# Reworking the head of a fused state-space and dense kernel: another load queue, a square root with a reciprocal, transposed tiles copied by two engines

## The chip, the cores and the metric

One core of one Trainium2 chip. Times are device microseconds of one execution. Every execution quoted here was undisturbed ("fast"). A kernel was timed in 4 to 6 executions, with 6 to 11 executions of the kernel before beside it. Ratios are the mean time of one kernel's fast runs over that of the kernel before in the same rounds, so they are not quite the ratio of the medians that stand beside them.

The device time is longer than the span of the trace (first to last instruction). The part outside the span hardly varies within a kernel: about 2.0 us for the kernel before.

## The reference, cut to what matters

```python
xn = layernorm(x)                                   # x: 1 x 2048 x 1024
# A: a diagonal state-space layer on xn; the recurrence over 2048 steps is complex
Bu = einsum("bld,pd->blp", xn, B_bar);  h_t = Lam_bar * h_(t-1) + Bu_t
A  = 2 * einsum("blp,dp->bld", h, C).real + xn * Dskip
# B: a dense layer with mish: 1024 -> 3584 -> 1024
Bo = mish(xn @ w1 + b1) @ w2
out = x + A + Bo
```

The output is bf16. The layernorm feeds both halves, so no useful matmul can start before the first rows are normalized and transposed.

## The kernel before

The program keeps one list of instructions for each engine, in program order, and derives semaphores from recorded reads and writes. The 2048 rows are done in four blocks of 512 rows. In each block PE does w1 (28 tiles `f`, 8 matmuls each), then the projection into the state (8 tiles `j`, 16 matmuls each), then w2 and the projection out. The first block also has to make what later blocks reuse: sine and cosine tables, transposed B and C, coefficients.

The head (rows `q` = 0 and 1 are the ones that the first half-width matmuls wait for):

```python
for q in range(NQ):
    load_x(SP, 0, q)                       # 4 tiles of 128 rows, all on SyncE's queue
# ... 4 small parameter rows on ScalarE's queue, then 7 weight tiles (512 KB each) on SyncE's ...
def first_rsqrt(q):                        # ScalarE: 1/sqrt estimate
    aop(lambda e: e.activation(rc(q, 1), mv[:, q, 1:2], AF.Abs_reciprocal_sqrt, ...))
def first_apply(q):                        # VectorE: one Newton step (3 small ops), then xn
    ...
keep_busy(34)                              # filler matmuls (0.107 us each, 0.056 us from 6.5 us on)
PE.op(... transpose of the parameter rows ...)
keep_busy(16)
# ... statistics of tile 0 on VectorE, of tile 1 on ScalarE ...
first_apply(0); first_transpose(0); keep_busy(6)
first_apply(1); first_transpose(1); keep_busy(8)
first_copy(0, VE); first_copy(1, VE)       # PSUM -> xnT, both on VectorE
```

GpSimd makes the phases of the sine tables, 24 instructions in a row, and in their middle issues the x tiles of the second block:

```python
for j in range(NJ):
    phases(j)        # px = iot*thp; py = round(px); xs = px - py: 128x512 fp32 each
    if j == 3:
        for q in range(NQ):
            load_x(PO, 1, q)               # block 1, GpSimd's queue
```

Of the kernel before, what the change touches and what calls it, by code (L numbers as in the profile page):

```python
# [5 lines left out]
ALU = mybir.AluOpType  # L6
AF = mybir.ActivationFunctionType
DT = mybir.dt

P = 128  # L10
# [146 lines left out]
def build_kernel(nc, A_x, A_Lambda_re, A_Lambda_im, A_B_re, A_B_im, A_C_re, A_C_im,  # L157
                 A_log_dt, A_Dskip, B_w1, B_b1, B_w2, out):
    bf16, f32, i32 = DT.bfloat16, DT.float32, DT.int32
    S, D = A_x.shape[1], A_x.shape[2]  # L160
# [4 lines left out]
    NQ = TB // P  # L165
    NK = D // P
    NJ = NP // P
    NF = F // P
# [4 lines left out]
    EPS = 1e-5  # L173

    PE = Queue(nc, "pe")
    VE = Queue(nc, "ve")
    AC = Queue(nc, "ac")
    PO = Queue(nc, "po")
    SP = Queue(nc, "sp")

    def sb(name, shape, dtype):
        return nc.alloc_sbuf_tensor(name, shape, dtype)
# [18 lines left out]
    hT = sb("hT", [P, 2, NJ, TB], bf16)  # L201
    b_hT = [[Buf("hT%d_%d" % (ci, j)) for j in range(NJ)] for ci in range(2)]
    xnT = sb("xnT", [P, NK, TB], bf16)
    b_xnT = [Buf("xnT%d" % q) for q in range(NQ)]
    s_xnT = [DmaSem(nc, "d_xnT%d" % q) for q in range(NQ)]
    tab = sb("tab", [P, 2, NJ, TB], bf16)
    b_tab = [Buf("tab%d" % j) for j in range(NJ)]
# [4 lines left out]
    xn = sb("xn", [P, NQ, D], bf16)  # L212
    b_xn = [Buf("xn%d" % q) for q in range(NQ)]
# [4 lines left out]
    NST = 3 * NJ + NF  # L218
    st = sb("st", [NST, P], bf16)
    b_st = Buf("st")  # L220
    ident = sb("ident", [P, P], bf16)
    b_ident = Buf("ident")
    par = sb("par", [P, NST], f32)
    b_par = Buf("par")
    stats = sb("stats", [P, 2, 2, 6], f32)
    b_stats = [Buf("stats%d" % i) for i in range(2)]
    mv = sb("mv", [P, NQ, 2], f32)
    b_mv = [Buf("mv%d" % i) for i in range(NQ)]
    rs = sb("rs", [P, NQ, 4], f32)
    b_rs, b_rs1, b_rs2 = ([Buf("rs%s%d" % (n, i)) for i in range(NQ)] for n in "abc")  # L230
    kon = sb("kon", [P, 3], f32)
    b_kon = Buf("kon")
    CN = ["dt", "a", "th", "thp", "r", "xs", "ys", "xc", "yc", "s1", "c1", "lr", "li", "nr",
# [15 lines left out]
    b_ps = [Buf("ps%d" % i) for i in range(8)]  # L249

    def ps16(i):
        return ps[:, i, :].bitcast(bf16)
# [23 lines left out]
    vop, aop, pop = VE.op, AC.op, PO.op  # L276


    s_st = DmaSem(nc, "d_st", nper=4)
# [4 lines left out]
    def load_x(queue, blk, q):  # L284
        r0 = blk * TB + q * P
        i = blk % 2
        queue.dma(lambda e: e.dma_start(xx[:, i, q, :], A_x[0, r0:r0 + P, :]),  # L287
                  s_xx[i][q] if blk else s_x0[q], writes=[b_xx[i][q]])

    for q in range(NQ):  # L290
        load_x(SP, 0, q)
    for src, r0, n in ((A_log_dt, 2 * NJ, NJ), (A_Lambda_im, NJ, NJ), (A_Lambda_re, 0, NJ),
                       (B_b1, 3 * NJ, NF)):
        AC.dma(lambda e, src=src, r0=r0, n=n: e.dma_start(
            st[r0:r0 + n, :], src.rearrange("(j p) -> j p", p=P)), s_st, writes=[b_st])


    items = []
# [27 lines left out]
                                  compare_op=ALU.is_equal, fill=0.0), reads=[b_ident], writes=[b_ident])  # L326
    for n, v in enumerate((HALF_PI, 0.0, EPS)):
        pop(lambda e, n=n, v=v: e.memset(kon[:, n:n + 1], v), reads=[b_kon], writes=[b_kon])
    pop(lambda e: e.iota(iot_i[:], pattern=[[1, TB]], base=0, channel_multiplier=0), writes=[b_iot_i])
    pop(lambda e: e.tensor_copy(iot[:], iot_i[:]), reads=[b_iot_i], writes=[b_iot])  # L330

# [4 lines left out]
    def rc(q, n):  # L336
        return rs[:, q, n:n + 1]

    def first_sums_v(q, h):
        s = q // 2  # L340
        vop(lambda e: e.bn_stats(stats[:, s, h, :], xx[:, 0, q, h * 512:(h + 1) * 512]),  # L341
            reads=[b_xx[0][q]], writes=[b_stats[s]])

    def first_var_v(q):
        s = q // 2
        vop(lambda e: e.bn_aggr(mv[:, q, :], stats[:, s, :, :]), reads=[b_stats[s]], writes=[b_mv[q]])
        vop(lambda e: e.tensor_scalar(rc(q, 0), mv[:, q, 1:2], EPS, None, op0=ALU.add),
            reads=[b_mv[q]], writes=[b_rs[q]])

    def first_mean_a(q):  # L350
        aop(lambda e: e.activation(sq[:], xx[:, 0, q, :], AF.Identity, bias=kon[:, 1:2], accum_out=rc(q, 3)),
            reads=[b_xx[0][q], b_kon], writes=[b_sq, b_rs[q]])
        aop(lambda e: e.activation(mv[:, q, 0:1], rc(q, 3), AF.Copy, scale=-1.0 / D),
            reads=[b_rs[q]], writes=[b_mv[q]])

    def first_var_a(q):
        aop(lambda e: e.activation(sq[:], xx[:, 0, q, :], AF.Square, bias=mv[:, q, 0:1], accum_out=mv[:, q, 1:2]),
            reads=[b_xx[0][q], b_mv[q]], writes=[b_sq, b_mv[q]])

    def first_rsqrt(q):  # L360
        scale = 1.0 if q % 2 == 0 else 1.0 / D
        aop(lambda e: e.activation(rc(q, 1), mv[:, q, 1:2], AF.Abs_reciprocal_sqrt, scale=scale, bias=kon[:, 2:3]),
            reads=[b_mv[q], b_kon], writes=[b_rs1[q]])

    def first_apply(q):

        v, y, t = (rc(q, n) for n in range(3))
        if q % 2:
            vop(lambda e: e.tensor_scalar(v, mv[:, q, 1:2], 1.0 / D, EPS, op0=ALU.mult, op1=ALU.add),
                reads=[b_mv[q]], writes=[b_rs[q]])  # L370
        vop(lambda e: e.scalar_tensor_tensor(out=t, in0=y, scalar=y, in1=v, op0=ALU.mult, op1=ALU.mult),  # L371
            reads=[b_rs[q], b_rs1[q]], writes=[b_rs2[q]])
        vop(lambda e: e.tensor_scalar(t, t, -0.5, 1.5, op0=ALU.mult, op1=ALU.add),
            reads=[b_rs2[q]], writes=[b_rs2[q]])
        vop(lambda e: e.tensor_tensor(y, y, t, op=ALU.mult), reads=[b_rs1[q], b_rs2[q]], writes=[b_rs1[q]])
        vop(lambda e: e.tensor_scalar(xn[:, q, :], xx[:, 0, q, :], mv[:, q, 0:1], y,  # L376
                                      op0=ALU.subtract if q % 2 == 0 else ALU.add, op1=ALU.mult),
            reads=[b_xx[0][q], b_mv[q], b_rs1[q]], writes=[b_xn[q]])

    def first_transpose(q):  # L380
        bank = 6 + q % 2
        for k in range(NK):
            PE.mm(lambda e, k=k: e.transpose(ps16(bank)[:, k * P:(k + 1) * P], xn[:, q, k * P:(k + 1) * P], ident[:]),  # L383
                  reads=[b_xn[q], b_ident], writes=[b_ps[bank]], first=k == 0, last=k == NK - 1)

    def first_copy(q, queue):
        dst = xnT[:, :, q * P:(q + 1) * P]
        srcp = ps16(6 + q % 2).rearrange("p (k t) -> p k t", k=NK)
        if queue is AC:
            aop(lambda e: e.copy(dst, srcp), reads=[b_ps[6 + q % 2]], writes=[b_xnT[q]])  # L390
        else:
            vop(lambda e: e.tensor_copy(dst, srcp), reads=[b_ps[6 + q % 2]], writes=[b_xnT[q]])  # L392


    rv = [sb("rv%d" % i, [P, NQ], f32 if i < 3 else i32) for i in range(4)]
# [60 lines left out]
    def keep_busy(n):  # L456
        for i in range(n):
            PE.mm(lambda e: e.matmul(ps[:, 4, 0:P], lhsT=ident[:], rhs=ident[:], start=True, stop=True),
                  reads=[b_ident], writes=[b_ps[4]], first=i == 0, last=i == n - 1)

    keep_busy(34)
    PE.op(lambda e: e.transpose(ps16(5)[:, 0:NST], st[:, :], ident[0:NST, 0:NST]),
          reads=[b_st, b_ident], writes=[b_ps[5]])
    keep_busy(16)
    aop(lambda e: e.activation(rs[:, :, 3], kon[:, 2:3].to_broadcast([P, NQ]), AF.Abs_reciprocal_sqrt, bias=kon[:, 2:3]),
        reads=[b_kon], writes=b_rs)
    for h in range(2):
        first_sums_v(0, h)
    first_var_v(0)
    first_sums_v(2, 0)  # L470
    first_mean_a(1)
    first_rsqrt(0)
    first_var_a(1)
    first_rsqrt(1)
    first_apply(0)
    first_transpose(0)
    keep_busy(6)
    first_apply(1)
    first_transpose(1)
    keep_busy(8)  # L480
    first_copy(0, VE)
    first_copy(1, VE)
    first_mean_a(3)
    first_var_a(3)
    first_rsqrt(3)
    first_sums_v(2, 1)
    first_var_v(2)
    first_rsqrt(2)
    first_apply(2)
    first_apply(3)  # L490
    vop(lambda e: e.tensor_copy(par[:, :], ps16(5)[:, 0:NST]), reads=[b_ps[5]], writes=[b_par])
    NSPLIT = 6

    def first_half(f, half):
        s, fi = f // 2, f % 2
        wt = ring[:, s, :].rearrange("p (k f) -> p k f", k=NK)
        ts = slice(half * 256, half * 256 + 256)
        for k in range(NK):
            PE.mm(lambda e, k=k: e.matmul(ps[:, f, ts], lhsT=wt[:, k, fi * P:(fi + 1) * P], rhs=xnT[:, k, ts],  # L499
                                          start=k == 0, stop=k == NK - 1),  # L500
                  reads=[b_ring[s]] + b_xnT[2 * half:2 * half + 2], writes=[b_ps[f]],
                  first=half == 0 and k == 0, last=half == 1 and k == NK - 1)

    for f in range(NSPLIT):
        first_half(f, 0)
        if f in (2, 3):
            q = f
            first_transpose(q)
            first_copy(q, AC if q == 2 else VE)

    aop(lambda e: e.activation(c("dt"), ldt, AF.Exp), reads=[b_par], writes=[b_cs["dt"]])
    small("a", "dt", lre, ALU.mult)
# [358 lines left out]
```

## Time and profile before

| what | before |
|---|---|
| median of the first 3 executions | 626.24 us (625.97 to 626.64) |
| span of the profiled one | 623.9 us |
| first useful matmul | 10.27 us |
| PE's only longer wait after it | 1.5 us, at 94.55 us |

From the page of the kernel before: the span, the busy time of the engines, the chain of work that ended last, and PE's group of w2 matmuls. In a group the columns are busy us and mean ns of one, then the idle time ahead of them and what ended it.

```profile
span 623.9 us, 7415 instructions
...
PE 616.7 (99%) x2961; PEld 287.4 (46%) x2961; DVE 466.0 (75%) x695; ACT 247.1 (40%) x162; POOL 50.0 (8%) x47
...
PE 95%; DVE 3%; DMA 1%; issue 0%; SPq 0%; DVEq 0%
...
L715 PE MATMUL ps<-ring,act 128*128 128x512 bf16 x896 | 194.2, 379 | 1.5 <-DVE mt L666 1.5
```

The last one: once, PE waits 1.5 us for VectorE.

The timeline of the head before (start, duration, engine, line, operation, output and inputs, idle time before it):

```profile
0.79 1.84 SPq L287 DMA_DIRECT2D xx<-in_A_x_dram  x4
...
1.41 3.81 PE L458 MATMUL ps<-ident 128*128 128x128 bf16 x34 [1.41 <-POOL kon L328]
...
6.81 0.55 DVE L376 TENSOR_SCALAR xn<-xx,mv,rs 128x1024 bf16<-128x1024 bf16 x1
...
7.41 0.62 PE L383 MATMUL ps<-ident,xn 128*128 128x128 bf16 x8 [0.50 <-DVE rs L369]
...
8.17 0.55 DVE L376 TENSOR_SCALAR xn<-xx,mv,rs 128x1024 bf16<-128x1024 bf16 x1
...
8.63 1.49 DVE L392 COPY xnT<-ps 128x1024 bf16<-128x1024 bf16 x2
...
8.77 0.62 PE L383 MATMUL ps<-ident,xn 128*128 128x128 bf16 x8 [0.40 <-DVE xn L376]
...
10.27 2.78 PE L499 MATMUL ps<-xnT,ring 128*128 128x256 bf16 x24 [0.43 <-DVE xnT L392]
```

Fillers, then xn0, its transposes, xn1, its transposes, two copies of 0.7 us, and the first useful matmul at 10.27 us.

### The profile page before, as it was taken

To read this page: it belongs to the slowest core of one execution; us is meant where nothing else is said; L and a number is where in the kernel's file an instruction comes from. 1 tells how busy PE (TensorE), PEld (TensorE's weight loads), DVE (VectorE), ACT (ScalarE), POOL (GpSimd) and SP (SyncE) were. 2 spreads that over 40 slices of the span, in tenths; PEclk is the share of its full clock that TensorE was granted. 3 is DMA by queue.
4 is the path that set the end of the run, shared out by engine and by line. 5 is a ranking of instruction groups with operands and counts; after the bars stand their busy time and mean duration, and the time that the engine had idled before them with its cause. 6 is when DMAs were issued, how large, how long until landed. Compare 5 with 4: busy or idle time off the path is not lost.

```text
span 623.9 us, 7415 instructions
## 1 busy us (share of the span) xinstructions
PE 616.7 (99%) x2961; PEld 287.4 (46%) x2961; DVE 466.0 (75%) x695; ACT 247.1 (40%) x162; POOL 50.0 (8%) x47
## 2 busy tenths in 40 slices
PE   8999999999999999999999999999999999999998
PEld 7644444444444444444444444444444444444443
DVE  6799999999457599999047759999624856999603
ACT  6679995441059950000008992000001999000000
POOL 1899000000100000000010000000000000000000
PEclk9999999999999999999999999999999999999999
DMA  9999976750365400764065520285204532033001
GB/s 268 215 259 249 258 152 172 200 166 3 106 198 169 134 2 7 232 171 132 13 190 144 159 101 1 77 227 153 85 35 134 167 137 68 1 131 106 1 0 68
DMA packets 124188, 79.41 MB, mean 127 GB/s; under 512 B 48890, under 2 KB 106490, under 8 KB 124154
## 3 DMA queue, kind: packets, MB, share of 16 engines
q1 hardware_dynamic: 120656, 71.58, 42.9%
q10 hardware_dynamic: 2538, 4.21, 1.8%
q0 software_dynamic: 960, 3.15, 1.8%
q8 instruction: 24, 0.39, 0.3%
q14 instruction: 10, 0.08, 0.0%
HBM read 63.19 MB, written 4.19 MB: 108 GB/s over the span
## 4 chain that ended last, share of the span: by engine, by line
PE 95%; DVE 3%; DMA 1%; issue 0%; SPq 0%; DVEq 0%
PE ps L715 48%; PE ps L641 29%; PE ps L661 16%; DVE mt L666 2%; PE ps L499 2%; DMA xx<-in_A_x_dram 1%; DVE hT L669 0%; PE ps L383 0%; DVE hT L671 0%; DVE xn L376 0%; SPq L287 0%; DVE xnT L392 0%; DVE xx L752 0%; DVE rs L371 0%; DVE stats L341 0%
## 5 line engine op out<-in xcount | busy, mean ns | idle before, releaser
L715 PE MATMUL ps<-ring,act 128*128 128x512 bf16 x896 | 194.2, 379 | 1.5 <-DVE mt L666 1.5
L641 PE MATMUL ps<-xnT,ring 128*128 128x512 bf16 x848 | 183.7, 379 | 0.0
L619 ACT ACTIVATE act<-hb 128x3584 bf16<-128x3584 bf16 x16 | 50.9, 3183 | 246.2 <-DVE hb L648 245.9
L715 PEld LDWEIGHTS ps<-ring,act 128*128 128x128 bf16 x896 | 87.5, 98 | 107.6 <-DVE mt L666 2.0
L641 PEld LDWEIGHTS ps<-xnT,ring 128*128 128x128 bf16 x848 | 82.9, 98 | 99.9
L648 DVE TENSOR_SCALAR hb<-ps,par 128x512 bf16<-128x512 f32 x112 | 82.8, 747 | 55.3 <-PE ps L641 54.0
L661 PE MATMUL ps<-xnT,BT 128*128 128x512 bf16 x512 | 111.2, 379 | 0.0
L715 PE MATMUL ps<-CT,hT 128*128 128x512 bf16 x512 | 111.2, 379 | 0.0
L666 DVE TENSOR_TENSOR mt<-ps,tab 128x1024 bf16<-128x1024 f32 x64 | 75.4, 1219 | 13.2 <-PE ps L661 11.7
L661 PEld LDWEIGHTS ps<-xnT,BT 128*128 128x128 bf16 x512 | 50.0, 98 | 60.5
L715 PEld LDWEIGHTS ps<-CT,hT 128*128 128x128 bf16 x512 | 50.0, 98 | 60.5
L752 DVE TENSOR_TENSOR xx<-ps,xx 128x1024 bf16<-128x1024 f32 (+1 forms) x17 | 19.5, 1161 | 72.0 <-PE ps L715 72.0
L681 DVE TENSOR_TENSOR_SCAN hT<-cs,qi,hT 128x512 bf16<-128x512 f32 x48 | 58.9, 1269 | 0.0
L621 ACT ACTIVATE act<-act 128x3584 bf16<-128x3584 bf16 x16 | 51.0, 3190 | 0.2
L620 ACT ACTIVATE act<-act 128x3584 bf16<-128x3584 bf16 x16 | 51.0, 3190 | 0.2
L686 DVE TENSOR_TENSOR mt<-hT,tab 128x1024 bf16<-128x1024 bf16 x64 | 41.4, 688 | 1.1
L626 DVE TENSOR_TENSOR act<-act,hb 128x3584 bf16<-128x3584 bf16 x16 | 32.3, 2017 | 1.3 <-ACT act L621 1.3
L287 POOL DMA_DIRECT2D xx<-in_A_x_dram x12 | 6.7, 559 | 254.8 <-DVE xx L752 250.5
L595 ACT ACTIVATE ct<-CT,cs 128x512 f32<-128x512 bf16 x16 | 11.5, 718 | 29.1 <-DVE CT L597 24.5
L620 ACT ACT_TABLE_LOAD x16 | 20.5, 1283 | 0.3
L621 ACT ACT_TABLE_LOAD x16 | 20.5, 1283 | 0.3
L681 DVE TENSOR_TENSOR_SCAN hT<-cs,hT 128x512 bf16<-128x512 f32 x16 | 18.7, 1208 | 0.0
(82 smaller groups left out, 280.2 us busy)
## 6 DMA issues: line engine op xcount, KB each, us to landing
ring<-in_B_w_dram SPq DMA_DIRECT2D x112, 512.0 KB, 3.7
out_dram<-xx ACTq DMA_DIRECT2D x15, 256.0 KB, 2.0
xx<-in_A_x_dram POOLq DMA_DIRECT2D x12, 256.0 KB, 4.0
xx<-in_A_x_dram SPq DMA_DIRECT2D x4, 256.0 KB, 3.4
dsk<-in_A_Dskip_dram SPq DMA_DIRECT2D x1, 256.0 KB, 6.4
out_dram<-xx ACTq DMA_DIRECT2D x2, 128.0 KB, 1.7
xnT<-xn SPq DMA_TRANSPOSE x12, 4.5
BT<-in_A_B_re_dram SPq DMA_TRANSPOSE x8, 5.9
```

Source lines behind the costliest of these rows:

```text
L619: aop(lambda e: e.activation(a, hs, AF.Exp), reads=[b_hb[g % 2]], writes=[b_act[g]])
L620: aop(lambda e: e.activation(a, a, AF.Ln, bias=1.0), reads=[b_act[g]], writes=[b_act[g]])
L621: aop(lambda e: e.activation(a, a, AF.Tanh), reads=[b_act[g]], writes=[b_act[g]])
L626: vop(lambda e: e.tensor_tensor(a, a, hs, op=ALU.mult), reads=[b_act[g], b_hb[g % 2]], writes=[b_act[g]])
L641: PE.mm(lambda e, k=k: e.matmul(ps[:, bank, :], lhsT=wt[:, k, fi * P:(fi + 1) * P], rhs=xnT[:, k, :], start=k == 0, stop=k == NK - 1), rea ...
L648: vop(lambda e: e.tensor_scalar(hb[:, hs, :], ps[:, bank, :], b1(f), None, op0=ALU.add), reads=[b_ps[bank], b_par], writes=[b_hbf[hs]])
L661: PE.mm(lambda e, j=j, ci=ci, k=k, bank=bank: e.matmul(ps[:, bank + ci, :], lhsT=BT[:, ci, j, k, :], rhs=xnT[:, k, :], start=k == 0, stop= ...
L666: vop(lambda e, s=s, u=u, j=j: e.tensor_tensor(mt[:, s, :, :], u, tab[:, s, j, :].unsqueeze(1).to_broadcast([P, 2, TB]), op=ALU.mult), rea ...
L681: vop(lambda e, ci=ci, init=init: e.tensor_tensor_scan(out=hT[:, ci, j, :], data0=cj("r", j).to_broadcast([P, TB]), data1=hT[:, ci, j, :], ...
L686: vop(lambda e, s=s: e.tensor_tensor(mt[:, s, :, :], hT[:, :, j, :], tab[:, s, j, :].unsqueeze(1).to_broadcast([P, 2, TB]), op=ALU.mult), ...
L715: PE.mm(lambda e: e.matmul(ps[:, u, :], lhsT=lhsT, rhs=rhs, start=st_, stop=last), reads=reads, writes=[b_ps[u]], first=st_, last=last)
L752: vop(lambda e: e.tensor_tensor(xr, src, xr, op=ALU.add), reads=b_src + [b_x], writes=[b_x])
```

## The change

The intent is an earlier first useful matmul: load tile 1 on its own queue, drop the Newton step by taking a square root on ScalarE and a reciprocal on VectorE, and let ScalarE and VectorE copy the two transposed tiles at once. The core of the diff:

```diff
-        load_x(SP, 0, q)
-    ... 4 parameter rows: AC.dma(...)
+        load_x(AC if q == 1 else SP, 0, q)
+    def load_rows(): ... 4 parameter rows: PO.dma(...)      # called after GpSimd's constants
@@
-        aop(... AF.Abs_reciprocal_sqrt, scale=scale, bias=kon[:, 2:3]) ...
+        aop(... AF.Sqrt, scale=scale, bias=kon[:, 2:3]) ...
@@ first_apply
-        3 small VectorE ops of a Newton step (4 for odd q)
+        vop(lambda e: e.reciprocal(y, y), ...)
@@
-    keep_busy(34)
-    PE.op(... transpose of the parameter rows ...)
-    keep_busy(16)
+    keep_busy(76)
@@
-    keep_busy(8)
-    first_copy(0, VE)
-    first_copy(1, VE)
+    keep_busy(4)
+    first_copy(0, AC)
+    first_copy(1, VE, 0, 4)          # tile 1 in two PSUM banks, half for each engine
+    first_copy(1, AC, 4, NK)
@@ after the first 8 useful matmuls
+            PE.op(... transpose of the parameter rows ...); vop(... copy to par ...)
-            first_copy(q, AC if q == 2 else VE)
+            first_copy(q, VE)
```

More of the change, by code (lines that the diff above doesn't have):

```diff
@@ L203, in build_kernel @@
     xnT = sb("xnT", [P, NK, TB], bf16)
-    b_xnT = [Buf("xnT%d" % q) for q in range(NQ)]
+    b_xnT = [Buf("xnT%d" % q, parts=[Buf("xnT%d_%d" % (q, h)) for h in range(2)]) for q in range(NQ)]
     s_xnT = [DmaSem(nc, "d_xnT%d" % q) for q in range(NQ)]
@@ L229, in build_kernel @@
     rs = sb("rs", [P, NQ, 4], f32)
-    b_rs, b_rs1, b_rs2 = ([Buf("rs%s%d" % (n, i)) for i in range(NQ)] for n in "abc")
+    b_rs, b_rs1 = ([Buf("rs%s%d" % (n, i)) for i in range(NQ)] for n in "ab")
     kon = sb("kon", [P, 3], f32)
@@ L290, in build_kernel, with load_rows @@
     for q in range(NQ):
-        load_x(SP, 0, q)
-    for src, r0, n in ((A_log_dt, 2 * NJ, NJ), (A_Lambda_im, NJ, NJ), (A_Lambda_re, 0, NJ),
-                       (B_b1, 3 * NJ, NF)):
-        AC.dma(lambda e, src=src, r0=r0, n=n: e.dma_start(
-            st[r0:r0 + n, :], src.rearrange("(j p) -> j p", p=P)), s_st, writes=[b_st])
+        load_x(AC if q == 1 else SP, 0, q)
+    def load_rows():
+        for src, r0, n in ((A_log_dt, 2 * NJ, NJ), (A_Lambda_im, NJ, NJ), (A_Lambda_re, 0, NJ),
+                           (B_b1, 3 * NJ, NF)):
+            PO.dma(lambda e, src=src, r0=r0, n=n: e.dma_start(
+                st[r0:r0 + n, :], src.rearrange("(j p) -> j p", p=P)), s_st, writes=[b_st])
     items = []
@@ L328, in build_kernel @@
         pop(lambda e, n=n, v=v: e.memset(kon[:, n:n + 1], v), reads=[b_kon], writes=[b_kon])
+    load_rows()
     pop(lambda e: e.iota(iot_i[:], pattern=[[1, TB]], base=0, channel_multiplier=0), writes=[b_iot_i])
@@ L346, in first_var_v @@
         vop(lambda e: e.bn_aggr(mv[:, q, :], stats[:, s, :, :]), reads=[b_stats[s]], writes=[b_mv[q]])
-        vop(lambda e: e.tensor_scalar(rc(q, 0), mv[:, q, 1:2], EPS, None, op0=ALU.add),
-            reads=[b_mv[q]], writes=[b_rs[q]])
     def first_mean_a(q):
@@ L358, in first_var_a, with first_sqrt @@
             reads=[b_xx[0][q], b_mv[q]], writes=[b_sq, b_mv[q]])
-    def first_rsqrt(q):
+    def first_sqrt(q):
         scale = 1.0 if q % 2 == 0 else 1.0 / D
-        aop(lambda e: e.activation(rc(q, 1), mv[:, q, 1:2], AF.Abs_reciprocal_sqrt, scale=scale, bias=kon[:, 2:3]),
+        aop(lambda e: e.activation(rc(q, 1), mv[:, q, 1:2], AF.Sqrt, scale=scale, bias=kon[:, 2:3]),
             reads=[b_mv[q], b_kon], writes=[b_rs1[q]])
     def first_apply(q):
-        v, y, t = (rc(q, n) for n in range(3))
-        if q % 2:
-            vop(lambda e: e.tensor_scalar(v, mv[:, q, 1:2], 1.0 / D, EPS, op0=ALU.mult, op1=ALU.add),
-                reads=[b_mv[q]], writes=[b_rs[q]])
-        vop(lambda e: e.scalar_tensor_tensor(out=t, in0=y, scalar=y, in1=v, op0=ALU.mult, op1=ALU.mult),
-            reads=[b_rs[q], b_rs1[q]], writes=[b_rs2[q]])
-        vop(lambda e: e.tensor_scalar(t, t, -0.5, 1.5, op0=ALU.mult, op1=ALU.add),
-            reads=[b_rs2[q]], writes=[b_rs2[q]])
-        vop(lambda e: e.tensor_tensor(y, y, t, op=ALU.mult), reads=[b_rs1[q], b_rs2[q]], writes=[b_rs1[q]])
+        y = rc(q, 1)
+        vop(lambda e: e.reciprocal(y, y), reads=[b_rs1[q]], writes=[b_rs1[q]])
         vop(lambda e: e.tensor_scalar(xn[:, q, :], xx[:, 0, q, :], mv[:, q, 0:1], y,
@@ L378, in first_apply, with bank_T, first_copy @@
             reads=[b_xx[0][q], b_mv[q], b_rs1[q]], writes=[b_xn[q]])
+    def bank_T(q, k):
+        if q == 1 and k >= NK // 2:
+            return 5
+        return 6 + q % 2
     def first_transpose(q):
-        bank = 6 + q % 2
         for k in range(NK):
-            PE.mm(lambda e, k=k: e.transpose(ps16(bank)[:, k * P:(k + 1) * P], xn[:, q, k * P:(k + 1) * P], ident[:]),
-                  reads=[b_xn[q], b_ident], writes=[b_ps[bank]], first=k == 0, last=k == NK - 1)
-    def first_copy(q, queue):
-        dst = xnT[:, :, q * P:(q + 1) * P]
-        srcp = ps16(6 + q % 2).rearrange("p (k t) -> p k t", k=NK)
+            bank = bank_T(q, k)
+            PE.mm(lambda e, k=k, bank=bank: e.transpose(ps16(bank)[:, k * P:(k + 1) * P],
+                                                        xn[:, q, k * P:(k + 1) * P], ident[:]),
+                  reads=[b_xn[q], b_ident], writes=[b_ps[bank]],
+                  first=k == 0 or bank != bank_T(q, k - 1), last=k == NK - 1 or bank != bank_T(q, k + 1))
+    def first_copy(q, queue, k0=0, k1=NK):
+        dst = xnT[:, k0:k1, q * P:(q + 1) * P]
+        bank = bank_T(q, k0)
+        srcp = ps16(bank).rearrange("p (k t) -> p k t", k=NK)[:, k0:k1, :]
+        b_dst = b_xnT[q] if k1 - k0 == NK else b_xnT[q].parts[k0 // 4]
         if queue is AC:
-            aop(lambda e: e.copy(dst, srcp), reads=[b_ps[6 + q % 2]], writes=[b_xnT[q]])
+            aop(lambda e: e.copy(dst, srcp), reads=[b_ps[bank]], writes=[b_dst])
         else:
-            vop(lambda e: e.tensor_copy(dst, srcp), reads=[b_ps[6 + q % 2]], writes=[b_xnT[q]])
+            vop(lambda e: e.tensor_copy(dst, srcp), reads=[b_ps[bank]], writes=[b_dst])
     rv = [sb("rv%d" % i, [P, NQ], f32 if i < 3 else i32) for i in range(4)]
@@ L459, in keep_busy @@
                   reads=[b_ident], writes=[b_ps[4]], first=i == 0, last=i == n - 1)
-    keep_busy(34)
-    PE.op(lambda e: e.transpose(ps16(5)[:, 0:NST], st[:, :], ident[0:NST, 0:NST]),
-          reads=[b_st, b_ident], writes=[b_ps[5]])
-    keep_busy(16)
-    aop(lambda e: e.activation(rs[:, :, 3], kon[:, 2:3].to_broadcast([P, NQ]), AF.Abs_reciprocal_sqrt, bias=kon[:, 2:3]),
-        reads=[b_kon], writes=b_rs)
+    keep_busy(76)
+    aop(lambda e: e.activation(rs[:, :, 3], kon[:, 2:3].to_broadcast([P, NQ]), AF.Sqrt), reads=[b_kon], writes=b_rs)
     for h in range(2):
@@ L469, in build_kernel @@
     first_var_v(0)
+    first_mean_a(1)
+    first_sqrt(0)
+    first_var_a(1)
+    first_sqrt(1)
     first_sums_v(2, 0)
-    first_mean_a(1)
-    first_rsqrt(0)
-    first_var_a(1)
-    first_rsqrt(1)
     first_apply(0)
@@ L479, in build_kernel @@
     first_transpose(1)
-    keep_busy(8)
-    first_copy(0, VE)
-    first_copy(1, VE)
-    first_mean_a(3)
-    first_var_a(3)
-    first_rsqrt(3)
+    keep_busy(4)
+    first_copy(0, AC)
+    first_copy(1, VE, 0, 4)
+    first_copy(1, AC, 4, NK)
     first_sums_v(2, 1)
     first_var_v(2)
-    first_rsqrt(2)
+    first_mean_a(3)
+    first_sqrt(2)
+    first_var_a(3)
+    first_sqrt(3)
     first_apply(2)
     first_apply(3)
-    vop(lambda e: e.tensor_copy(par[:, :], ps16(5)[:, 0:NST]), reads=[b_ps[5]], writes=[b_par])
     NSPLIT = 6
@@ L505, in build_kernel @@
         first_half(f, 0)
+        if f == 0:
+            PE.op(lambda e: e.transpose(ps16(5)[:, 0:NST], st[:, :], ident[0:NST, 0:NST]),
+                  reads=[b_st, b_ident], writes=[b_ps[5]])
+            vop(lambda e: e.tensor_copy(par[:, :], ps16(5)[:, 0:NST]), reads=[b_ps[5]], writes=[b_par])
         if f in (2, 3):
```

## The prediction

> **What bounds the kernel.** TensorE. The page gives PE 99% busy of a 623.9 us span and 95% of the chain that ended last. Listing the matmul starts in the timeline, only four steps are longer than a normal one: three in the head (at 7.41, 8.77 and 10.27 us) and one at 94.55 us, 1.5 us, where PE waits for VectorE's mt tile. VectorE has no idle piece over 0.15 us from 28.75 us past 94 us, but that chain is started by PE's own tiles, so it shifts with the head. So only the time of the first useful matmul (10.27 us) can move, and whatever it moves goes 1:1 into the end. The change touches the first 16 us of 624: even deleting a fifth of the head would be 0.3%.
>
> **The head before, from the timeline.** x0 lands 3.47, x1 4.21, x2 5.55 us. VectorE's Newton chain (0.20+0.15+0.16 us plus gaps) gives xn0 at 7.36 and xn1 at 8.72 us; transposes start 7.41 and 8.77; VectorE copies the two tiles at 8.63 (0.68) and 9.43 (0.69); first matmul 10.27. The filler matmuls before the transposes end at 6.75, so they don't bind.
>
> **What the change does.**
> - x1 issued at 0.8 instead of 1.25 us, x2 0.45 us earlier; ScalarE's table load starts about 1.4 instead of 2.43 us. x1 about 3.8, sqrt1 about 7.0 instead of 7.35.
> - Newton step gone, one reciprocal (0.15 to 0.2 us by the 128x8 one in the trace) in its place: about 0.5 us less for each tile. I expect xn0 at about 6.8 and xn1 at about 7.75 us, 0.6 and 1.0 us earlier.
> - Fillers before the first transpose: 76 instead of 50, and they stand in PE's order. In the trace a filler takes 0.107 us until 6.45 us, 0.056 us after it (the page's granted clock turns full there). 47 slow and 29 fast ones from 1.41 us end at 8.05 us. So the first transposes start at about 8.05, LATER than before (7.41), with xn0 waiting 1.2 us for PE. The second start at 8.84.
> - Copies: ScalarE does tile 0 (1.01 us, as its copy in the trace), then half of tile 1 (about 0.6) one after the other: 8.7 to 9.7 to 10.3 us. VectorE's half (0.4) is done at 9.65. So "at once" is in fact bound by 1.6 us of ScalarE in series, against 1.4 us of VectorE before.
> - First useful matmul about 10.4 us; the little parameter transpose now follows it (+0.06). Tiles 2 and 3 become ready just in time (about 12.9 and 14.4 us), at most 0.1 us of new wait.
>
> Net: +0.1 to +0.2 us. [...]
>
> **Prediction:** 626.3 us, 8 in 10 between 625.5 and 627.2. Faster by over 2%: 0.003; within 2%: 0.994; slower by over 2%: 0.003.
>
> **Right if** the timeline shows no PE gap ahead of the first transpose, xn0 written over 0.5 us before it, the first ps<-xnT,ring matmul between 9.6 and 11 us, and the same 1.5 us wait near 94.5 us. **Wrong if** the clock turns full much earlier or later; if x0 and x1, loaded side by side, land over 0.5 us later; if the parameter rows, now on the GpSimd queue, land after 10.5 us and hold PE; or if tile 3 comes late.

The sum: 10.4 us for the first useful matmul in place of 10.27, net +0.1 to +0.2 us on the 626.24 us of before, so about 626.3 us.

## More of the kernel before

SyncE's queue feeds weight tiles (a ring of 7) and transposes B and C by DMA, in one order:

```python
if f % 2 == 1: ring_load()                 # next 512 KB weight tile
if f < 16 and f % 2 == 0: transpose_B(f // 2)     # 2 x 256 KB
```

VectorE reads the projected tiles out of PSUM, and a product of 2.0 us (the mish of group 2) stands ahead of the last of them:

```python
def project_in(blk):
    for j in range(NJ):
        # 16 matmuls into two PSUM banks, then VectorE: two mt products, two sums
        if j == (6 if blk == 0 else 4):
            mish_mul(2)
```

## The result and the profile after

| | before | after |
|---|---|---|
| median | 626.12 us (625.74 to 626.64, 6 runs) | 626.95 us (625.88 to 628.31, 6 runs) |
| ratio of fast runs | | 1.0015, 95% interval 1.0001 to 1.0029 |
| span of the profiled execution | 623.9 us | 624.2 us |
| first useful matmul | 10.27 us | 9.83 us |

Well within 2%, and slower by the medians; the interval only just leaves out 1. The spread is wider in these six executions (2.4 us against 0.9), but the kernel before reached 628.61 and 631.13 us in later rounds, so a wider spread is not established. The head became faster. The profiled execution of the changed kernel is the shortest of its six (625.88 us), so its trace shows the loss at its smallest: its span is 0.3 us longer than that of the execution profiled before (626.0 us), though its device time is 0.1 us shorter. The spans of the other five are 624.8 to 626.6 us; what made them longer stands in no trace.

From the page of the changed kernel, the lines that answer to those above:

```profile
span 624.2 us, 7389 instructions
...
PE 88%; SPq 5%; DVE 2%; ACT 2%; DMA 1%; issue 1%; DVEq 0%
...
L717 PE MATMUL ps<-ring,act 128*128 128x512 bf16 x880 | 193.4, 379 | 2.5 <-DVE mt L668 1.6
```

SyncE's queue now holds 5% of the chain. (This trace lacks some matmul records, so 2.5 us of idle time holds gaps that are missing records; the 1.6 us put down to VectorE are real.) The head in the timeline:

```profile
0.79 1.35 SPq L287 DMA_DIRECT2D xx<-in_A_x_dram  x3
0.80 0.40 ACTq L287 DMA_DIRECT2D xx<-in_A_x_dram  x1
...
1.41 6.08 PE L460 MATMUL ps<-ident 128*128 128x128 bf16 x76 [1.41 <-POOL kon L330]
...
6.44 0.55 DVE L369 TENSOR_SCALAR xn<-xx,mv,rs 128x1024 bf16<-128x1024 bf16 x1
...
7.33 0.61 PE L381 MATMUL ps<-ident,xn 128*128 128x128 bf16 x8
...
7.88 0.55 DVE L369 TENSOR_SCALAR xn<-xx,mv,rs 128x1024 bf16<-128x1024 bf16 x1
7.98 1.01 ACT L392 COPY xnT<-ps 128x1024 bf16<-128x1024 bf16 x1 [0.41 <-PE ps L381]
...
8.49 0.62 PE L381 MATMUL ps<-ident,xn 128*128 128x128 bf16 x8 [0.21 <-DVE xn L369]
...
9.14 0.58 ACT L392 COPY xnT<-ps 128x512 bf16<-128x512 bf16 x1 [0.15 <-PE ps L381]
...
9.83 1.03 PE L497 MATMUL ps<-xnT,ring 128*128 128x256 bf16 x8 [0.50 <-ACT xnT L392]
```

The first transposes follow the fillers with no gap (7.33 us; xn0 was done at 6.99), and ScalarE's second copy releases the first useful matmul, 0.44 us earlier than before. That copy did not follow straight on ScalarE's first one: it waited 0.15 us for the transposes of tile 1, and these had waited 0.21 us for xn1. So in this execution tile 1's statistics set the first useful matmul, not the fillers and not two copies in series. Half of the gain is gone soon: the parameter transpose, now in PE's way at 10.79 us, costs 0.22 us (eight matmuls of 0.109 us end at 10.70, the ninth starts at 10.92), and the last half-width matmul starts at 21.32 us against 21.53 before.

Where does that go? I put the starts of the same VectorE instructions of both traces side by side. The bias adds (hb<-ps,par) mark the progress of the first block:

| instruction | before, us | after minus before |
|---|---|---|
| bias add 1 | 17.57 | -0.30 |
| bias add 10 | 28.75 | -0.20 |
| bias add 15 | 43.45 | +0.42 |
| bias add 24 | 62.33 | +0.27 |
| last mt product of the projection | 93.28 | +0.27 |
| last output add | 620.96 | +0.27 |

So the gain is 0.2 us at 28.75 us, a loss of 0.27 us at 62 us, and from there to the end nothing changes. In both traces VectorE does not wait for PE between bias add 10 and the projected tiles (no idle piece over 0.15 us): in that stretch VectorE is the bound, and PE's wait near 94.5 us is where PE pays for it. From bias add 10 to bias add 24 VectorE took 33.59 us before and 34.06 us after, for the same instructions.

The timeline of VectorE and GpSimd near 30 us, first before, then after:

```profile
29.68 0.37 DVE L448 TENSOR_TENSOR cs<-cs 128x8 f32<-128x8 f32 x2
30.08 0.39 DVE L452 TENSOR_SCALAR cs<-cs 128x8 f32<-128x8 f32 x2
30.23 0.69 DVE L430 TENSOR_TENSOR mt<-xn,dsk 128x1024 bf16<-128x1024 bf16 x1
30.52 1.53 POOL L525 TENSOR_TENSOR ph_h<-px,py 128x512 f32<-128x512 f32 x1
30.96 1.64 DVE L432 TENSOR_TENSOR xx<-xx,mt 128x1024 bf16<-128x1024 bf16 x1
```

```profile
29.48 0.37 DVE L450 TENSOR_TENSOR cs<-cs 128x8 f32<-128x8 f32 x2
29.68 1.31 POOL L527 TENSOR_TENSOR ph_h<-px,py 128x512 f32<-128x512 f32 x1
...
29.88 1.20 DVE L454 TENSOR_SCALAR cs<-cs 128x8 f32<-128x8 f32 x2
31.00 0.68 DVE L432 TENSOR_TENSOR mt<-xn,dsk 128x1024 bf16<-128x1024 bf16 x1
31.08 2.03 POOL L523 TENSOR_SCALAR px<-iot,cs 128x512 f32<-128x512 f32 x1
```

Before, the pair of tiny scaling operations took 0.39 us; after, 1.20 us, because GpSimd's subtraction started 0.2 us ahead of it, and it ends within 0.1 us of that subtraction's end. Before, the same subtraction met a VectorE operation of another kind, which took 1.64 us. The clearest case is at 61 us before: a VectorE operation on 128x4 elements, 0.16 us elsewhere, took 1.25 us, from 0.04 us after GpSimd's last subtraction started to 0.02 us after it ended. The next bias add, the twenty-fourth, could start only then:

```profile
61.12 1.27 POOL L525 TENSOR_TENSOR ph_a<-px,py 128x512 f32<-128x512 f32 x1
61.16 1.25 DVE L418 TENSOR_TENSOR rv<-rv 128x4 f32<-128x4 f32 x1
...
62.33 0.74 DVE L648 TENSOR_SCALAR hb<-ps,par 128x512 bf16<-128x512 f32 x1
```

Which operations are held differs between GpSimd's instructions. Over these two traces, four small VectorE operations (128x4 or 128x8, at most 0.17 us where no GpSimd arithmetic ran) began 0.04 to 0.5 us after the start of a subtraction (1.3 us in most cases). All four took 0.8 to 1.26 us and were done 0.02 to 0.03 us after that subtraction's end; one that began 0.005 us after a subtraction's start took its 0.17 us. Under the scaling and rounding (1.6 and 1.9 us in most cases) it was otherwise: of 58 small operations that began during one of them, 48 took 0.3 us or less, and of the ten others seven were done 0.62 to 0.72 us after its start. (The spans of GpSimd instructions are rough.)

So the loss is a matter of which GpSimd instruction meets which VectorE instruction. That gave the theories for the experiments.

### The profile page after: what moved, and what is told of

Its sections match the earlier page's. It is cut to its first block, busy times and chain, and to the rows that moved or that the text cites. A ratio compares the mean times of both kernels' runs of the same rounds, so it can differ in the third digit from the quotient of the medians.

```text
span 624.2 us, 7389 instructions
## 1 busy us (share of the span) xinstructions
PE 614.3 (98%) x2927; PEld 288.3 (46%) x2983; DVE 463.7 (74%) x683; ACT 247.5 (40%) x163; POOL 52.5 (8%) x51
## 4 chain that ended last, share of the span: by engine, by line
PE 88%; SPq 5%; DVE 2%; ACT 2%; DMA 1%; issue 1%; DVEq 0%
PE ps L717 48%; PE ps L643 21%; PE ps L663 18%; SPq L608 4%; PE ps L497 1%; DVE mt L668 1%; DMA ring<-in_B_w_dram 1%; DMA xx<-in_A_x_dram 1%; ACT act L623 1%; ACT act L621 1%; ACT act L622 1%; SPq L318 1%; DVE hb L650 0%; DVE act L628 0%; PE ps L381 0%
```

## The experiments

Theories, in the order in which they came up:

- **A**: the 76 fillers tie the first useful matmul to the moment at which PE's clock turns full, which differs between executions: 6.48 us in the trace before, 4.95 us in the one after.
- **B**: VectorE's chain, stretched by GpSimd, takes the head's gain back.
- **C**: weight tiles land late near 50 to 59 us, after SyncE's stream has stalled behind GpSimd's x transfers.
- **D**, a sharper B: what counts is how much earlier GpSimd's phase arithmetic starts relative to VectorE's chain.

### Fewer fillers

```diff
-    keep_busy(76)
+    keep_busy(50)
```

> The changed kernel with 50 fillers ahead of the first transposes in place of 76, nothing else. Theory A (76 fillers in PE's order make the first useful matmul follow the moment at which the clock turns full, which differs from run to run): the runs close up to within about 0.8 us of each other (they spread 2.4 us with 76), the median falls from 626.95 to about 626.0 us, and the first ps<-xnT,ring matmul stays near 9.8 us because ScalarE's second copy sets it. Theory B (the head's gain is lost later, in VectorE's chain, stretched by GpSimd, and in ring loads that come late near 56 us; fillers don't matter): median and spread stay as they are, about 626.9 us and over 1.5 us.

Measured: 627.31 us (625.82 to 628.08), ratio 1.0009 (0.9993 to 1.0024). The first useful matmul came at 9.79 us, as expected, but neither the median nor the spread shrank. Theory A does not explain the changed kernel. The trace shows another loss. In the waits of PE in this kernel, from 18 to 100 us (total, times, longest):

```profile
PE ps L643 <- DMA ring<-in_B_w_dram: 2.8, 3, 1.3
```

and in SyncE's queue in the timeline of the same execution:

```profile
36.80 2.24 POOL L287 DMA_DIRECT2D xx<-in_A_x_dram  x4
...
37.69 1.76 SPq L608 DMA_TRANSPOSE BT<-in_A_B_im_dram  x1
...
39.54 0.53 SPq L318 DMA_DIRECT2D ring<-in_B_w_dram  x1
...
40.11 8.00 SPq L608 DMA_TRANSPOSE BT<-in_A_B_re_dram  x1
...
48.15 1.63 SPq L608 DMA_TRANSPOSE BT<-in_A_B_im_dram  x1
```

The weight tile issued at 39.54 landed at 50.08 us, and PE waited for it: one transpose stood 8.00 us at its issue, while the four x tiles of the second block were under way on GpSimd's queue. Between 40 and 46 us SyncE's queue moved 0.26 MB here, 0.66 MB in the kernel before, while GpSimd's moved 0.74 and 0.77 MB. This is theory C; the cause of the stall was not settled. It costs more than the 1.5 us that PE loses near 94 us anyway, and this execution took 1.4 us more than the one before by its span.

### The kernel before with more fillers

```diff
-    keep_busy(16)
+    keep_busy(42)
```

> The kernel before with the second group of fillers raised from 16 to 42 (76 in all, and the parameter transpose), the rest of the head as before. Theory A: the first transposes now wait for the fillers in the executions in which the clock turns late; the median rises by 0.1 to 0.8 us and the spread grows to over 1.2 us (from 0.9). Theory B: same as before, 626.1 us, spread as before.

Measured: 626.48 us (626.22 to 627.77), ratio 1.0003 (0.999 to 1.0016). In its trace the clock turned full late, at 7.47 us; the first transposes started at 8.65 and the first useful matmul at 10.91 us, so fillers do bind in such an execution, as theory A says. Over all executions the effect (0.35 us between medians) is inside the interval. In this trace the first useful matmul is 0.64 us later than before, and so is everything after it up to the last output add (621.60 against 620.96 us). Here a shift of the head does go 1:1 into the end, and GpSimd, which waits for the same parameters, has shifted along with VectorE.

### One product moved out of VectorE's way, in both kernels

```diff
-            if j == (6 if blk == 0 else 4):
+            if j == (7 if blk == 0 else 4):
                 mish_mul(2)
```

> The kernel before with one VectorE product of 2.0 us (act<-act,hb of group 2 in the first block) moved from ahead of the last projected tile to behind it; same work, other order. Both theories: PE's one wait of 1.5 us near 94.5 us shrinks to 0.3 us or less and the time falls by 1.2 to 1.5 us, to about 624.8 us, if VectorE's chain is what sets the end of that stage. If PE alone had set it, nothing changes.

> The changed kernel with the same product moved. Theory B (VectorE's chain took the head's gain back): with VectorE out of the way the changed kernel becomes faster than the kernel before with the same move, by 0.2 to 0.4 us, so about 624.5 us, and its spread falls under 1 us. Theory A (fillers and clock): it stays 0.3 to 0.9 us slower than the other and spreads over 1.5 us, 625.2 to 625.8 us.

Measured: before 624.47 us (624.07 to 626.66), ratio 0.9975 (0.9959 to 0.9991); changed 624.55 us (624.24 to 626.98), ratio 0.9976 (0.9958 to 0.9994). PE no longer waits for VectorE near 94 us in either trace. So VectorE's chain was what set that moment: 1.66 us by the medians (626.13 less 624.47), for the order of one instruction. This is more than the whole head change could give. Between the two kernels neither theory's difference appeared, nor did the spread fall under 1 us (2.6 and 2.7 us); the changed one's trace has two waits for weight tiles, 1.4 us together, theory C again.

### The second block's x tiles on SyncE's queue

```diff
-                load_x(PO, 1, q)
+                load_x(SP, 1, q)
```

(with semaphores of their own). They are then issued behind the first seven weight tiles, at about 14 us.

> The changed kernel with one thing else: the four x tiles of the second block (1 MB) are issued from SyncE's queue at about 14 us, behind the first weight tiles, in place of GpSimd's queue at 37 us. Theory C (the extra time and spread of the changed kernel come from this: while GpSimd's x transfers are under way, SyncE's stream of transposes and weight tiles all but stops, for 4 to 9 us; weight tiles 11 to 13 then land late and PE waits near 50 to 59 us, longer than VectorE's lag hides): the stop is gone, weight tile 13 lands over 2 us ahead of its use, the median falls to 625.9 us (plus or minus 0.3) and the spread to under 1 us. Rival B (VectorE's chain, stretched by GpSimd's arithmetic): median stays near 626.9 us with a spread over 1.5 us.

> The same edit in the kernel before. Theory C: its median stays at 626.0 us (VectorE's chain, 1.5 us wait of PE near 94 us, bounds it either way), but its rare long runs (626.6 to 628.6 us) go: spread under 0.8 us. Rival B: nothing changes.

Measured: changed 626.52 us (625.74 to 629.0), ratio 1.0007 (0.9979 to 1.0034); before 625.88 us (625.49 to 626.05), ratio 0.9986 (0.9961 to 1.0012). In the kernel before none of six executions was over 626.05 us, as theory C expected, where 4 of 11 without the edit were over 626.5 us in the same rounds; six are too few to be sure. In the changed kernel the weight tiles came in time in the trace (tile 13 lands 1.9 us ahead of its use, less than the 2 us expected), yet the median and the spread (3.3 us) missed what theory C expected: late tiles alone do not account for the loss. That they have a share is not excluded. The waits of PE in that trace:

```profile
PE ps L718 <- DVE mt L669: 2.2, 1, 2.2
```

VectorE was late by more than before, and a second loss followed the wait. Windows of this kernel, then of the kernel before (us, busy time and count of PE, PEld, DVE, ACT, POOL, granted clock, DMA share, GB/s):

```profile
93.00:96.00 3.00, 0.81 (x4) 0.13 (x2) 2.96 (x5) 2.99 (x2) 0.00 (x0) 0.94 0.00 0
96.00:99.00 3.00, 3.00 (x8) 1.06 (x7) 2.97 (x5) 2.05 (x4) 0.00 (x0) 0.50 0.00 0
```

```profile
93.00:96.00 3.00, 1.48 (x8) 0.70 (x8) 2.97 (x5) 3.00 (x3) 0.00 (x0) 1.00 0.00 0
96.00:99.00 3.00, 3.00 (x16) 1.37 (x14) 2.93 (x5) 1.02 (x2) 0.00 (x0) 1.00 0.50 173
```

After the wait of 2.2 us the clock was at half for 3.4 us: 8 matmuls in 3 us in place of 16, a loss of about 1.7 us (half of 3.4). The column PE busy shows 3.00 in both; only the clock and the counts tell. Executions with a mean granted clock of 0.997 or less are mostly among the longest: one of 628.31 us of the changed kernel, and 628.64 and 629.0 us of this one; the kernel before has them too (628.61 and 631.13 us in other rounds).

### Both edits in both kernels

> The changed kernel with both walls taken away: x tiles of the second block on SyncE's queue, and the 2.0 us product moved behind the last projected tile. Both theories together: PE waits nowhere past 15 us over 0.3 us; time 624.0 us (plus or minus 0.3), 0.2 to 0.45 us below the kernel before with the same two edits, which is the gain of the head as its trace shows it at 14 to 20 us.

> The kernel before with the same two edits: 624.3 us (plus or minus 0.3), spread under 0.8 us (with the product moved alone it was 624.47 with runs up to 626.66).

Measured: changed 625.02 us (624.62 to 625.17), ratio 0.9973 (0.9949 to 0.9996); before 624.11 us (623.92 to 624.92), ratio 0.9961 (0.9938 to 0.9985). The second is as expected. The first misses by 1.0 us: with the late weight tiles gone and 2 us of room for VectorE, the changed kernel is still 0.9 us slower. PE waits 0.5 us for VectorE in it, and 0.2 us lie outside the span. This miss led to theory D. The starts in all ten traces at hand fall into two families:

| kernels | GpSimd's first px ahead of bias add 10 | bias add 10 to 24 |
|---|---|---|
| before, its product moved, its 76 fillers | 12.01 us each | 33.58 to 33.59 us |
| before with x on SyncE, alone and with the product moved | 12.01 us | 33.43 us |
| changed, its 50 fillers, its product moved | 12.65 to 12.66 us | 34.06 to 34.08 us |
| changed with x on SyncE, alone and with the product moved | 12.65 to 12.66 us | 34.25 to 34.26 us |

The change lets GpSimd start 0.64 us earlier relative to VectorE, since the parameters reach it earlier: its chain starts at 15.89 us, before at 16.74. In the traces ScalarE no longer copies tile 2 (before, from 13.53 to 14.54 us), so its first operation on the parameters starts at 14.06 us instead of 15.86. The time of the first useful matmul does not show this.

### GpSimd started later

```diff
     turns()
+    pop(lambda e: e.iota(iot_i[:], pattern=[[1, TB]], base=0, channel_multiplier=0),
+        reads=[b_cs["thp"]], writes=[b_iot_i])          # writes the same numbers again
     for j in range(NJ):
         phases(j)
```

> The changed kernel, with one more GpSimd instruction (an index fill of about 0.6 us that nothing needs) ahead of its chain of phase arithmetic. In all five traces of the family before, that chain starts 12.01 us ahead of VectorE's tenth bias add and VectorE then takes 33.4 to 33.6 us to the twenty-fourth; in all five of the changed family it starts 12.65 us ahead and VectorE takes 34.1 to 34.3 us. Theory D (the two engines' relative start alone makes the difference, by the waits of one for the other): 12.0 us again and 33.6 us or less, PE's wait near 94 us back to 1.5 us or less, the median 0.4 to 1.0 us below the changed kernel's 626.95, so about 626.2 us; ring waits near 50 to 59 us may remain. Rival: the VectorE time stays at 34.1 us, whatever the start, and the median stays near 626.9 us.

Measured: 625.52 us (625.27 to 625.88), ratio 0.9987 (0.9975 to 1.0000), where the unchanged changed kernel had 1.0015. GpSimd starts 12.24 us ahead (not quite the 12.0 expected), VectorE takes 33.58 us, and every VectorE instruction from bias add 10 to the end runs 0.10 to 0.12 us ahead of the kernel before. PE's wait is back at what it was. Bias adds 10 and 24, and that wait:

```profile
28.64 0.75 DVE L652 TENSOR_SCALAR hb<-ps,par 128x512 bf16<-128x512 f32 x1 [0.54 <-PE ps L645]
...
62.21 0.74 DVE L652 TENSOR_SCALAR hb<-ps,par 128x512 bf16<-128x512 f32 x1
```

```profile
PE ps L719 <- DVE mt L670: 1.5, 1, 1.5
```

One useless instruction on an idle engine takes the changed kernel's loss away; its ratio and that of the changed kernel, each against the kernel before in its own rounds, have intervals that just do not overlap (1.0000 and 1.0001). That it beats the kernel before is not clear of noise: the interval reaches 1.0000, and 0.3 us of the 0.65 us between these medians lie outside the span. VectorE's part is theory D's result. The median fell further (1.4 us) than VectorE's 0.48 us explains. None of its five executions was over 625.88 us; the changed kernel had five over 626.5 us. I take the rest to be executions with late weight tiles or half clock, which the longer lag makes more frequent, but only single traces show those, so this share is argued, not shown. The added instruction also moves GpSimd's x transfers from 36.84 to 37.24 us, and no run separates that rival.

### GpSimd's arithmetic taken away

```diff
-        pop(... px = iot * thp ...); pop(... py = round(px) ...); pop(... xs = px - py ...)
+        pop(lambda e: e.memset(xs[:], 0.125), reads=[b_cs["thp"]], writes=[b_xs])
```

on top of x on SyncE's queue. The tables are wrong.

> Wrong result on purpose: the changed kernel with x on SyncE's queue, and GpSimd's 24 arithmetic instructions of the phases replaced by 8 fills that read nothing. Theory D: VectorE's long instructions (0.16 us ones that took 1.25 us) are gone, tenth to twenty-fourth bias add takes 31 us or less, and though the product of 2.0 us still stands ahead of the last projected tile, PE waits under 0.3 us near 94 us; time about 624.3 us. Rival (VectorE is that slow by itself): 34 us and 626.5 us as with GpSimd's arithmetic.

Measured: 624.35 us (624.05 to 624.57), ratio 0.9967 (0.9952 to 0.9983), as expected. Bias add 10 to 24 takes 29.37 us, 4.9 us less than the 34.25 us of the same kernel with the arithmetic, and PE waits 0.05 us near 94 us with the product where it was. The operation that took 1.64 us before is at its own speed in this timeline:

```profile
30.63 0.69 DVE L435 TENSOR_TENSOR xx<-xx,mt 128x1024 bf16<-128x1024 bf16 x1
```

PE waits 0.5 us for a weight tile instead. The comparison with the reference is blind to these tables.

### Everything together

> The changed kernel with 50 fillers, GpSimd's chain started later, the second block's x tiles on SyncE's queue and the product moved behind the last projected tile. If the list of causes is complete: no PE wait over 0.3 us after 15 us, 623.8 us (plus or minus 0.3), 0.1 to 0.5 us below the 624.11 us of the kernel before with the last two edits, spread under 0.8 us. If GpSimd's start was not a cause, it stays at 625.0 us as without it.

> The same as the one with all four edits, and the second block's inverse square root with two Newton steps in place of three (0.8 us of small VectorE work less): a try at the best version. 623.7 us, at most 0.2 us below the one with three steps, since PE no longer waits for VectorE there; a median lower by 0.5 us or more would mean that VectorE still bounds that stage in most executions.

Measured: 624.21 us (624.15 to 625.81), ratio 0.9971 (0.9958 to 0.9983), and with two Newton steps 624.14 us (623.92 to 626.18), ratio 0.9973 (0.9959 to 0.9986). The 0.9 us gap to the kernel before with both edits is gone, so GpSimd's start belonged on the list (the fillers were changed with it, but changed nothing when alone); but in the medians the expected 0.1 to 0.5 us in favour of the new head did not appear. By the spans it did: the median is 622.1 us, against 622.3 us for the kernel before with both edits (on another chip), but 2.1 us lie outside the span here and 1.8 us there. The first one's trace, its longest execution (span 623.7 us; the other four had 622.0 to 622.1), shows a loss that remains in some:

```profile
PE ps L646 <- DMA ring<-in_B_w_dram: 1.5, 1, 1.5
```

Weight tile 13 landed at 57.64 us, needed near 56. Over the 14 traces it landed between 54.6 and 59.2 us, for uses that would come at about 56: a second wall just behind the first, also with x on SyncE's queue. A shorter head would only reach it sooner. What makes it vary between executions of one kernel stays open, as does which part of the SyncE stall is due to GpSimd's transfers.

The best versions, 624.11 us (the kernel before with two edits), 624.14 and 624.21 us, beat both kernels by about 2 us. They were timed on different chips and their intervals overlap; nothing here ranks them.

## Why the prediction was right or wrong

The time (626.95 us) lies in the range (625.5 to 627.2 us), above the stated 626.3; "within 2%" held. The reasons were half wrong. That it came out slower, as predicted, was luck: the small loss was expected in the head, which gained, and the loss arose where none was expected.

- **Load and statistics.** Tile 1 was to land at 3.8 us on its own queue; it landed at 4.26 us (before 4.21), and tile 0 at 4.09 (before 3.47). Two queues did not make two loads faster. The busy share of the DMA engines was 0.68 from 1.7 to 3 us and 1.04 from 3 to 4 us (before 0.86 and 0.95); what set the landings, no run separates. xn0 was done at 6.99 us (6.8 predicted) and xn1 at 8.43 (7.75 predicted).
- **Fillers.** Right that they precede the first transposes with no gap and that their end depends on the clock's turn. The size was off: they followed each other every 0.107 us up to 4.91 us and every 0.056 us from 4.99 us (before, up to 6.45 and from 6.53 us), so they ended at 7.33, not 8.05 us. The trace's record of the full clock begins at 4.95 us here and at 6.48 us before, 3.5 and 5.1 us after the first filler; with the turn at 7.47 us, in the kernel before with 76 fillers, the first transposes started at 8.65 us. At 7.33 us the fillers no longer set the first useful matmul: the transposes of tile 1 waited for xn1.
- **Copies.** The sizes were right (ScalarE 1.01 and 0.58 us, VectorE's half 0.42 us), and ScalarE's second copy is the one that releases the first useful matmul. But the two did not stand one after the other: ScalarE was idle for 0.15 us between them, so 1.6 us in series was not the bound.
- **First useful matmul.** 10.4 us predicted, 9.6 to 11 us as the mark of "right"; 9.83 us in the trace, 9.7 to 10.5 us in the six traces with this head, against 10.25 to 10.74 us in the four with the old one. So the head gained, where I expected a small loss. The parameter transpose behind it cost 0.22 us, not 0.06.
- **The step that failed:** "that chain is started by PE's own tiles, so it shifts with the head" and "whatever it moves goes 1:1 into the end". VectorE's chain is not of constant length. It contains several microseconds of waiting for GpSimd's instructions (4.9 us less without them), and the change moved GpSimd by 0.64 us relative to it, which made it 0.48 us longer. Of the loss this accounts for what the trace shows, 0.27 us at the end, and not for all of the 0.83 us between the medians. I had seen the 1.5 us wait and VectorE's gapless stretch, and still treated PE as the bound.
- **Spread.** It grew in these six executions, but not surely: the kernel before spread as widely in other rounds. With 50 fillers it stayed at 2.3 us. Late weight tiles (2.8 us of waits with 50 fillers) and half clock for 3.4 us after a wait of 2.2 us (x on SyncE's queue), each seen in a trace, are two sources.
- **The prediction's own tests.** Two marks of "right" held: no gap ahead of the first transpose, and the first useful matmul within 9.6 to 11 us. The wait near 94 us was 1.6 us in place of 1.5. One mark failed: xn0 was written 0.34 us before the first transpose, not over 0.5. One mark of "wrong" was met: tile 0 landed 0.62 us later; and the clock turned full 1.5 us earlier than in the trace before. These moved terms of the head's sum, but the error that counted came after the head.

## What to carry to other kernels

Before shortening a head, find which engine has no idle time up to the next wait of the bounding engine, and ask whether its length can change; here it was VectorE's, and the order of one instruction in it was worth more than the head. When one engine can hold up another, compare the durations of equal instructions between the traces, not only gaps, since a stretched instruction counts as busy (here one of 0.16 us that took 1.25 us). An edit that starts an idle engine earlier can cost more than it saves, so follow a gain of a few tenths of a microsecond to the end of the trace before you believe it.
